# Turning x and xn by VectorE squares and DRAM instead of TensorE, in an adaLN block of linear attention and MLP

## The chip, the cores and the metric

The kernel runs on one core of one Trainium2 chip. The metric is the device time of one execution in microseconds (us); the median of several runs is given. About the profile: PE is TensorE's matmul, PEld its weight load (they overlap), DVE is VectorE, ACT ScalarE, POOL GpSimd, SP SyncE, whose queue issues the DMAs.

## The reference

One block with 2048 tokens and D = 576, 32 heads of 18, and an MLP of F = 4608:

```python
mod = (silu(c) @ w_mod)                      # six pieces: sa, ca, ga, sb, cb, gb
h = layernorm(x) * (1 + ca) + sa
q, k, v = split(h @ wqkv)                    # per head
pq, pk = phi(q), phi(k)                      # phi(t) = (t + 1 if t > 0 else exp(t)) + 1e-6
o = (pq @ (pk.T @ v)) / (pq @ sum(pk) + 1e-6)
x = x + ga * (o @ wo)
h = layernorm(x) * (1 + cb) + sb
x = x + gb * (silu(h @ w1) @ w2)
```

## The kernel before

Tokens are handled in 16 tiles of 128 (index `t`) and in 4 blocks of 512 (index `tb`); features in five chunks `k`, four of 128 and one of 64 columns, which is doubled to 128 by a copy of its columns (the "tail"). Every fp32 operand of a matmul is split into a high and a low fp32r part (a cast on ScalarE, a subtraction `sub_hi`, L121, on VectorE), and three passes are summed.

A matmul needs h with the features on partitions, and LayerNorm needs tokens on partitions, so each block of h is turned once. `transpose_chunk` (L214) does it on TensorE: four transposes of 128x128 against an identity for a chunk, into one bank of PSUM; then ScalarE applies shift and scale on the way out (`modulate`, L199), casts the high part (L205, L1093 or L869), and VectorE subtracts.

**First part (to about 206 us): projections.** After a head (0 to 40 us: the modulation's columns, LayerNorm and turning of block 0 of x), a loop over `t` runs `k_proj`, `v_proj`, `q_proj` (L226) and `kv_mm` (L589). In block `tb` it prepares block `tb + 1`: `load_x` (L260) loads four tiles with one DMA each at `t % 4 == 0`; statistics (L178), reciprocal deviation (L184 on POOL, L185) and normalisation (L191 on ScalarE for odd tiles, L193 on VectorE for even) at 1; `turn(tb + 1, k)` turns the chunks at 2 and 3, into `hT[tb + 1]`. `mod_piece` and `mod_col` (L526) make the later modulation. `load_wo` runs at `t == 10`.

**Second part (206 to about 368 us): attention output and the first group of the MLP.** `attn_step` (divide by the norm, turn, multiply by the folded kv and wo, add x, which was reloaded into `acc` by L756) goes over the 16 tiles; when a block is complete, its rows are normalised (`xn`, L191 and L193), and `turn_all(tb)` turns them by `turn_chunk_k` (L214), makes sums and differences of pairs of blocks (a seven-product scheme), splits them and stores them to DRAM (`hd`, L962). `mlp_units` (L886, L897) computes the MLP's first group of 256 hidden columns from each block and fills TensorE between.

**Steady state (from about 368 us):** the other 17 groups, with operands streamed back from `hd`, weights loaded and split, `up` matmuls (L1324), `down` matmuls (L1397) and VectorE additions (L1405). It runs in an order written in the code.

The order of the rest is given by `ORDERS`: for each engine a list of instruction numbers in program order, which `arrange` turns into dependencies of each instruction on the one before it. TensorE's list is nearly the program's own order.

## Time and profile before

| | |
|---|---|
| timed runs (3) | 1137.52, 1137.76, 1138.51 us; median 1137.76 |
| span of the profiled execution, first to last instruction | 1136.9 us |
| matmuls | 7033 |
| DMA packets, bytes | 58813, 269.03 MB |
| transposes on TensorE: of x blocks 1 to 3, of xn | 60, 80 |

Busy shares are given by the profile for each engine; a matmul's end is modelled, so neighbours overlap and a busy time for a group counts each instant once. A group's row reads: line, engine, operation, output and inputs by the program's names, shapes, count, then busy time and mean duration of one in ns, then the engine's idle time before such instructions and what ended it. In a row of stretches each engine's busy time is followed by the number of its instructions, and at the end stand TensorE's granted clock, the mean busy share of the 16 DMA engines and GB/s. A row of waits reads: total us, times, longest. A row of the timeline reads: start, duration (of several merged instructions the whole), engine, line, operation, count.

### The profile page before, as it was taken

Reading aid. Unit: us, or ns where it says so; the run is one execution under the profiler, and the core shown is the slowest. Engines: PE = TensorE matmul, PEld = TensorE weight load, DVE = VectorE, ACT = ScalarE, POOL = GpSimd, SP = SyncE. Lnnn points to the kernel's source line nnn. Section 1 sums busy time; section 2 is a strip of 40 time slices with the busy share of each in tenths; the row PEclk is TensorE's granted clock in tenths of the full one; section 3 lists DMA queues with packets and bytes.
Section 4 is the critical chain, followed back from the end, with each engine's and each line's share of the span. In section 5 each row is a group of like instructions: output and inputs, shape, how many; then the busy total and the mean of one; then the engine's idle time right before and its main releaser. Section 6 shows DMA issues by size and latency. Waiting matters only on the chain.

```text
span 1136.9 us, 19287 instructions
## 1 busy us (share of the span) xinstructions
PE 1126.8 (99%) x7033; PEld 1040.8 (92%) x7033; DVE 971.0 (85%) x1543; ACT 538.7 (47%) x1112; POOL 649.3 (57%) x743
## 2 busy tenths in 40 slices
PE   8999999999999999999999999999999999999998
PEld 7999999999998899999999999999989999999998
DVE  6866744686878899999999999999999999999996
ACT  5643442547556544445445444444444444444441
POOL 1100000374714777767775776677667767776786
PEclk9999999999999999999999999999999999999999
DMA  9621100223359877976978869779778697697684
GB/s 281 199 84 31 44 7 1 71 84 116 137 198 354 340 274 256 348 278 257 361 261 315 314 250 356 273 255 364 261 277 331 265 344 281 258 346 274 256 310 156
DMA packets 58813, 269.03 MB, mean 237 GB/s; under 512 B 5724, under 2 KB 21856, under 8 KB 35680
## 3 DMA queue, kind: packets, MB, share of 16 engines
q1 hardware_dynamic: 58708, 267.80, 64.4%
q8 instruction: 56, 0.92, 0.3%
q14 instruction: 37, 0.30, 0.1%
q10 hardware_dynamic: 12, 0.00, 0.0%
HBM read 250.12 MB, written 16.78 MB: 235 GB/s over the span
## 4 chain that ended last, share of the span: by engine, by line
PE 94%; DMA 3%; DVE 1%; ACT 1%; POOL 0%; SPq 0%; issue 0%; POOLq 0%
PE up L1324 34%; PE down L1397 32%; PE psK L226 12%; PE big L226 7%; PE small L886 2%; PE big L897 2%; PE kvp L589 1%; DMA hT<-in_w_mod_dram 1%; PE big L812 1%; DMA raw<-in_w_mod_dram 1%; DMA hT<-hd 1%; PE small L214 1%; DMA xt<-in_A_x_dram 1%; PE up L1427 1%; PE down L1427 1%; PE psT L214 1%
## 5 line engine op out<-in xcount | busy, mean ns | idle before, releaser
L1405 DVE TENSOR_TENSOR acc<-down,acc 128x576 f32<-128x576 f32 x330 | 246.2, 754 | 13.2 <-PE down L1397 3.2
L1324 PE MATMUL up<-hT,w 128*128 128x512 f32 x916 | 239.4, 390 | 0.5 <-DMA hT<-hd 0.5
L1324 PEld LDWEIGHTS up<-hT,w 128*128 128x128 f32 x916 | 164.5, 188 | 25.4 <-DMA hT<-hd 0.7
L1359 POOL TENSOR_TENSOR s<-f,f 128x256 f32<-128x256 f32 x66 | 52.3, 792 | 159.7 <-ACT f L1340 159.7
L1397 PE MATMUL down<-w,hb 128*128 128x288 f32 x792 | 120.6, 294 | 0.0
L1397 PE MATMUL down<-w,hc 128*128 128x288 f32 x792 | 120.6, 294 | 0.0
L1397 PEld LDWEIGHTS down<-w,hc 128*128 128x128 f32 x792 | 113.7, 188 | 5.4 <-PE up L1324 0.3
L1397 PEld LDWEIGHTS down<-w,hb 128*128 128x128 f32 x792 | 113.7, 188 | 5.3
L121 DVE TENSOR_TENSOR w<-v,w 128x288 fp32r<-128x288 f32 (+1 forms) x170 | 114.8, 684 | 2.8 <-ACT w L1058 2.8
L1405 DVE TENSOR_TENSOR U<-down,U 128x576 f32<-128x576 f32 x132 | 99.6, 754 | 17.1 <-PE down L1397 15.2
L226 PE MATMUL psK<-w,hT 128*128 128x352 f32 (+3 forms) x506 | 106.4, 336 | 1.1 <-POOL w L317 0.6
L1324 PE MATMUL up<-room,w 128*128 128x512 f32 x348 | 91.0, 390 | 0.0
L1378 POOL TENSOR_TENSOR hc<-s,hc 128x512 fp32r<-128x512 f32 x66 | 89.4, 1355 | 0.1
L184 POOL TENSOR_TENSOR rstd<-ve,neghalf 128x4 f32<-128x4 f32 (+3 forms) x10 | 9.5, 953 | 138.8 <-DVE ve L183 138.8
L226 PEld LDWEIGHTS psK<-w,hT 128*128 128x128 f32 x506 | 81.8, 188 | 7.5 <-POOL w L317 0.8
L1340 ACT ACTIVATE f<-f 128x512 f32<-128x512 f32 x102 | 64.5, 632 | 47.8 <-DVE f L1345 24.8
L1343 DVE TENSOR_TENSOR f<-up,p 128x512 f32<-128x512 f32 x102 | 69.7, 683 | 12.1 <-PE up L1324 11.2
L1066 ACT CAST w<-v 128x288 fp32r<-128x288 f32 x85 | 36.7, 434 | 76.4 <-PE down L1397 62.1
L1324 PEld LDWEIGHTS up<-room,w 128*128 128x128 f32 x348 | 62.5, 188 | 9.4
L1363 POOL TENSOR_TENSOR f<-f,s 128x256 f32<-128x256 f32 x66 | 51.2, 776 | 34.9 <-DVE hb L1378 24.5
L1397 PE MATMUL down<-w,he 128*128 128x288 f32 x396 | 63.0, 294 | 0.0
L1397 PE MATMUL down<-w,ha 128*128 128x288 f32 x396 | 63.0, 294 | 0.0
(310 smaller groups left out, 2529.7 us busy)
## 6 DMA issues: line engine op xcount, KB each, us to landing
hT<-hd SPq DMA_DIRECT2D x66, 1280.0 KB, 5.5
hT<-hd SPq DMA_DIRECT2D x45, 1024.0 KB, 5.5
room<-hd SPq DMA_DIRECT2D x35, 1280.0 KB, 5.7
room<-hd SPq DMA_DIRECT2D x20, 1024.0 KB, 5.1
v<-in_B_w_dram SPq DMA_DIRECT2D x17, 576.0 KB, 7.2
v<-in_B_w_dram SPq DMA_DIRECT2D x17, 512.0 KB, 7.1
hd<-S SPq DMA_DIRECT2D x6, 1024.0 KB, 3.8
xt<-in_A_x_dram SPq DMA_DIRECT2D x16, 288.0 KB, 5.2
```

Of the source, the lines that this page charges most:

```text
L121: return V.tensor_sub(lo, full, f32(hi))
L214: T.transpose(ps[:, i * P : (i + 1) * P], xt[i][:, cidx * P : (cidx + 1) * P], ident)
L226: T.matmul(ps, xpart(a), wpart(b), start=n == 0, stop=n == len(XW) - 1)
L1066: A.copy(self.w2[n][:, 0], src)
L1324: T.matmul(ps, left, right, start=first and m == 0, stop=m == len(seq) - 1, skip_group_check=True)
L1340: A.activation(self.f[i, k], self.f[i, k], AF.Silu)
L1343: V.tensor_add(f, self.bank[bank[1]], self.p1)
L1359: G.tensor_add(self.s[:, 0:1], half(i, 0, 1), half(i, 1, 1))
L1363: G.tensor_sub(half(i, 1, 0), half(i, 1, 0), self.s[:, 1:2])
L1378: eng.tensor_sub(t[:, :, 1, :], src, f32(t[:, :, 0, :]))
L1397: T.matmul(ps[:, p, :HALF], self.a[i, n][:, u, p * P : (p + 1) * P], self.w.w2[n][:, v], start=n in (1, 5, 7, 6) and j == 0, stop=j == 2, ...
L1405: V.tensor_add(dst, ps[:, :, :HALF], dst)
```

## The change

**x, blocks 1 to 3.** `load_x` loads each tile in four DMAs of 32 rows, so that partition group `a` of tile `i` holds rows `a*128 + 32*i` to `+31` of the block. After the normalisation (without the tail copy; ScalarE does all of block 1 and the odd tiles of the others) VectorE transposes squares of 32x32, one instruction of 128x576 for a tile, and four DMAs write the block to DRAM, feature by feature, in runs of 128 tokens (512 bytes). `turn` then loads a chunk's rows of 512 tokens (the tail chunk twice, 64 rows each), which lie in the block's own order, and modulates and splits as before. The staging rooms lie in `acc`'s tiles 8 to 15, now parts of one tile; therefore `load_wo` moves from `t == 10` to 12, and wq's split ahead of `v_proj(1)`.

**xn, blocks 0 to 2.** ScalarE normalises all four tiles, VectorE transposes each by squares, four DMAs write the block, and `turn_chunk_k` loads chunks instead of turning them. Here the tokens come in the order (partition group, tile, place), and the views `nat` and `box` put them back in the cast and the subtraction. Block 3 still goes through TensorE. Its sums with the others need the same order, so its modulation writes through these views.

**mod_col** multiplies by 32 columns of ones instead of 128.

**Orders.** The `ORDERS` of all engines are new for everything up to the steady state, TensorE's too, where matmuls of neighbouring steps now alternate. (`manual_schedule` for TensorE becomes `nullcontext`, with the table in its place.)

```diff
-            0-106 114 107-109 115 110-113 116-2586
+            0-1 37 2-7 9-13 38 14 8 39 15-16 40 17 41 21 18-19 42 22 25 20 26 29-36 51 43 45 44 46 49-50 47 56 48 57
...
-    accb = [accp.tile([P, 4, D], F32, name=f"acc{b}") for b in range(NB)]
-    acc = [accb[t // 4][:, t % 4, :] for t in range(NT)]
+    acca = accp.tile([P, NT, D], F32, name="acc")
+    accb = [acca[:, 4 * b : 4 * b + 4] for b in range(NB)]
+    acc = [acca[:, t, :] for t in range(NT)]
...
-        nc.sync.dma_start(xt[:, :D], x[(tb * 4 + i) * P : (tb * 4 + i + 1) * P, :])
+        if tb == 0:
+            nc.sync.dma_start(xt[:, :D], x[i * P : (i + 1) * P, :])
+        else:
+            for a in range(4):
+                r0 = tb * 512 + a * P + 32 * i
+                nc.sync.dma_start(xt[32 * a : 32 * a + 32, :D], x[r0 : r0 + 32, :])
...
-            T.matmul(ps[:, k * P : (k + 1) * P], t[:, k * P : (k + 1) * P], ones, start=True, stop=True)
+            T.matmul(ps[:, k], t[:, k * P : (k + 1) * P], ones[:, :32], start=True, stop=True)
...
+    free = acca[:, QB : NT, :].rearrange("p t d -> p (t d)")
+    squares = free[:, : 4 * D].rearrange("p (b i j) -> p b i j", i=4, j=32)
+    places = [free[:, (KC + 1 + n) * 512 :][:, :512] for n in range(4)]
+    xd = [dram.tile([D, 512], F32, name=f"xd{n}") for n in range(1 + NB)]
+
+    def turn_squares(xts):
+
+        for i in range(4):
+            V.transpose(squares[:, :, i, :], xts[i][:, :D].rearrange("p (b j) -> p b j", j=32))
+        for a in range(4):
+            rows = slice(32 * a, 32 * a + 32)
+            nc.sync.dma_start(xd[NB][:, a * P : a * P + P].rearrange("(b j) t -> j b t", j=32),
+                              squares[rows].rearrange("j b i t -> j b (i t)"))
+
+    def load_turned(dst, src, k):
+        if k < KC:
+            nc.sync.dma_start(dst, src[k * P : (k + 1) * P, :])
+        else:
+            for h in range(2):
+                nc.sync.dma_start(dst[h * 64 : h * 64 + 64], src[KC * P : D, :])
+
     def turn(tb, k):
-        ps = psT()
-        transpose_chunk(xts, k, ps)
-        h32 = pa.tile([P, 512], F32, name="h32")
-        modulate_split(ps, k, hT[tb], cols["a"], h32)
+        h32 = places[CHUNKS.index(k)] if k != 3 else pa.tile([P, 512], F32, name="h32")
+        load_turned(h32, xd[NB], k)
+        modulate_split(h32, k, hT[tb], cols["a"], h32)
...
-                    ln.normalise(j, xts[j], xts[j], A if j % 2 else V)
+                    ln.normalise(j, xts[j], xts[j], A if tb == 0 or j % 2 else V, False)
+                turn_squares(xts)
...
-            if t == 10:
+            if t == 12:
                 load_wo()
...
+    def nat(t):
+        return t.rearrange("p (a i j) -> p i a j", a=4, i=4)
+
+    def box(t):
+        return t.rearrange("p (i a j) -> p i a j", a=4, i=4)
...
     def turn_chunk_k(tb, k, h32):
-        ps = small()
-        transpose_chunk(xn2[tb], k, ps)
-        modulate(ps, k, None, cols["b"], h32, A)
+        if tb in SQUARES:
+            ps = h32
+            load_turned(h32, xd[tb], k)
+        else:
+            ps = small()
+            transpose_chunk(xn2[tb], k, ps)
...
-            hi, lo = hpart(tb, k, 0), hpart(tb, k, 1)
-            return A.copy(hi, h32), sub_hi(lo, h32, hi)
-        return tail_h(htail(tb), h32)
+            hi, lo = box(hpart(tb, k, 0)), box(hpart(tb, k, 1))
+            return A.copy(hi, nat(h32)), sub_hi(lo, nat(h32), hi)
+        return tail_h(box(htail(tb)), nat(h32))
...
+                y = pb.tile([P, D], F32, name="prod")
+                lns[tb].normalise(i, y, acc[4 * tb + i], A, False)
+                V.transpose(y4[:, :, i, :], y.rearrange("p (b j) -> p b j", j=32))
+            if tb in SQUARES:
+                for n in range(4):
+                    rows = slice(32 * n, 32 * n + 32)
+                    nc.sync.dma_start(xd[tb][:, n * P : n * P + P].rearrange("(b j) t -> j b t", j=32),
+                                      y4[rows].rearrange("j b i t -> j b (i t)"))
```

Three places in the order show what moved. TensorE at tile 2 of the first part, between its key projection (`psK_618` before, `psK_631` after) and its value projection (`psK_665`, `psK_673`); `xt_394` to `xt_400` are the four tiles of x block 1. Before:

```order
L226 MATMUL psK_618<-w_106,hT_102 128x352
L226 MATMUL psK_618<-w_106,hT_102 128x288
L214 MATMUL psT_656<-ident_85,xt_394 128x128
L214 MATMUL psT_656<-ident_85,xt_396 128x128
L214 MATMUL psT_656<-ident_85,xt_398 128x128
L214 MATMUL psT_656<-ident_85,xt_400 128x128
L226 MATMUL psK_665<-w_103,hT_102 128x512
```
The same place after, where `kvp` is the product of keys and values of an earlier tile:

```order
L668 MATMUL kvp0_105<-pk0_147,vx0_149 128x256
L299 MATMUL psK_631<-w_103,hT_99 128x352
L299 MATMUL psK_631<-w_103,hT_99 128x288
L299 MATMUL psK_673<-w_100,hT_99 128x512
L299 MATMUL psK_673<-v_101,hT_99 128x512
L299 MATMUL psK_673<-w_100,hT_99 128x512
L668 MATMUL kvp2_107<-pk0_147,vx0_149 128x128
L299 MATMUL psK_673<-w_100,hT_99 128x512
```
The four transposes are gone, and the kv products stand between the projections' matmuls instead of behind them.

VectorE, where the last step of x block 1's chunks stands, the subtraction that fills the low half of its `hT` (`hT_490` before, `hT_513` after). Before:

```order
L121 TENSOR_TENSOR hT_490<-h32_788,hT_490 128x512
L121 TENSOR_TENSOR pk1_151<-a_774,pk1_151 128x576
L121 TENSOR_TENSOR vx1_153<-psK_792,vx1_153 128x4x126
L121 TENSOR_TENSOR hT_490<-h32_816,hT_490 128x512
L334 SCALAR_TENSOR_TENSOR acc0_95<-e_732,acc0_95 128x576
L178 BN_STATS st_1030<-xt_863 128x6 x2
```
After, with `xt_853` to `xt_868` the tiles of block 2:

```order
L258 SCALAR_TENSOR_TENSOR nm_1031<-mv_1028,rstd_1030 128x4
L266 TENSOR_SCALAR xt_853<-xt_853,mv_1028,rstd_1030 128x576
L720 STREAM_TRANSPOSE acc_95<-xt_853 128x18x32
L266 TENSOR_SCALAR xt_863<-xt_863,mv_1028,rstd_1030 128x576
L193 TENSOR_TENSOR vx1_150<-psK_786,vx1_150 128x4x126
L720 STREAM_TRANSPOSE acc_95<-xt_863 128x18x32
L193 TENSOR_TENSOR vx1_150<-psK_786,vx1_150 128x8
L193 TENSOR_TENSOR hT_513<-acc_95,hT_513 128x512
L720 STREAM_TRANSPOSE acc_95<-xt_858 128x18x32
L193 TENSOR_TENSOR hT_513<-acc_95,hT_513 128x512 x2
```
Block 1's subtractions stood ahead of block 2's statistics; now they stand behind its statistics and its first two transposes.

SP in the second part, at xn block 2 (`hd` is where the MLP's operands are stored; `acc` is reloaded with x). Before:

```order
L756 DMA acc_98<-in_A_x_dram 128x576
L962 DMA hd_2343<-hT 128x512
L962 DMA hd_2339<-S 128x2048
L756 DMA acc_98<-in_A_x_dram 128x576
L962 DMA hd_2342<-S 128x2048
L962 DMA hd_2343<-S 128x2048
L962 DMA hd_2346<-hT 128x2560
```
After, with `xd2_388` the room in DRAM:

```order
L856 DMA acc_95<-in_A_x_dram 128x576
L1342 DMA xd2_388<-xn_3363 32x18x128 x4
L1062 DMA hd07_2314<-S_3297 128x2048
L728 DMA H_3562<-xd2_388 128x512
L731 DMA ht_3563<-xd2_388 64x512
```
Four writes and the loads back (six for a block) are new, and the loads stand ahead of reloads of x and of stores to `hd`.

More of the change, by code (lines that the diff above doesn't have):

```diff
@@ L1 @@
-from contextlib import ExitStack
+from contextlib import ExitStack, nullcontext
 from itertools import count
@@ L185, in finish, with normalise @@
             V.scalar_tensor_tensor(nm, self.mv[:, a:b, 0], -1.0, rstd, op0=ALU.mult, op1=ALU.mult)
-        def normalise(self, i, xt, r, eng):
-            for o, lo, hi in ((D, KC * P, D), (0, 0, D)):
+        def normalise(self, i, xt, r, eng, tail=True):
+            for o, lo, hi in ((D, KC * P, D), (0, 0, D))[not tail :]:
                 dst, src, rstd = xt[:, o : o + hi - lo], r[:, lo:hi], self.rstd[:, i : i + 1]
@@ L412, in warm_up @@
             T.matmul(o[:, 0:P], ones, ones, start=True, stop=True)
-    with tc.manual_schedule(engines={mybir.EngineType.PE}):
+    with nullcontext():
         V.memset(ones, 1.0)
@@ L537 @@
     NP0 = 2
+    QB = NT // 2
     def xsel(t):
@@ L648 @@
                 k_proj(t)
+            if t == 1:
+                for k in START:
+                    split_w(wqp_, k, acc[10 + k], V)
             if more and i == 1:
@@ L665 @@
                 turn_half((4,))
-                for k in START:
-                    split_w(wqp_, k, acc[10 + k], V)
             if more and i >= 2:
@@ L687 @@
                 tm = mod_piece(t // 3)
-            if t == 10:
+            if t == 12:
                 load_wo()
-    with tc.manual_schedule(engines={mybir.EngineType.PE}):
+    with nullcontext():
         qs = iter(range(QB, NT))
@@ L847, in load_mlp @@
         return w1, w2, wt
-    DIFF, ODD = 9, 5
+    DIFF, ODD, SQUARES = 9, 5, (0, 1, 2)
     h2 = {}
@@ L1547 @@
     units = [(g, p) for g in range(1, NG) for p in range(2)]
-    with tc.manual_schedule(engines={mybir.EngineType.PE}):
+    with nullcontext():
         fetch(5)
```

172 lines of the change are left out of this document (125 added, 47 removed).

## The prediction

> **What bounds the kernel now.** I read first the page's busy times, then who waited for whom on TensorE, then the busy times in four stretches: the head, the projections, the attention with the first MLP pair, and the rest.
>
> ```profile
> span 1136.9 us, 19287 instructions
> PE 1126.8 (99%) x7033; PEld 1040.8 (92%) x7033; DVE 971.0 (85%) x1543; ACT 538.7 (47%) x1112; POOL 649.3 (57%) x743
> ```
> ```profile
> PE psK L407 <- ACT hT L205: 1.3, 1, 1.3
> ...
> PE small L214 <- ACT H L199: 0.4, 1, 0.4
> ```
> ```profile
> core 0: us, PE busy (x) PEld busy (x) DVE busy (x) ACT busy (x) POOL busy (x), PEclk, DMA share, GB/s
> 0.00:40.00 40.00, 35.54 (x247) 33.28 (x248) 29.36 (x72) 27.22 (x55) 8.40 (x16) 1.00 0.79 240
> 40.00:206.00 166.00, 165.42 (x1084) 155.90 (x1083) 101.30 (x198) 66.63 (x133) 5.95 (x9) 1.00 0.19 56
> 206.00:368.00 162.00, 160.59 (x1139) 153.66 (x1139) 126.00 (x222) 96.51 (x173) 81.23 (x77) 1.00 0.46 161
> 368.00:1136.00 768.00, 765.30 (x4569) 697.98 (x4567) 714.30 (x1054) 348.34 (x752) 553.72 (x642) 1.00 0.78 292
> ```
> TensorE is busy for all but 10 us; its longest wait is 1.3 us, the longest before a transpose 0.4 us; its clock is full in every stretch. So work taken off TensorE shortens the kernel by its own length, as long as nothing that TensorE reads comes later than now. From 40 to 368 us, where the edits lie (the head only gets a new order), VectorE is busy for 101.30 of 166 and 126.00 of 162 us, ScalarE for less, and the DMA engines for 0.19 and 0.46 of the time: there is room. The steady state after 368 us has none on VectorE (714 of 768), but its instructions stay the same.
>
> **The part removed.** The transposes through TensorE, alone, in the same two stretches:
>
> ```profile
> core 0: us, PE busy (x) PEld busy (x), PEclk, DMA share, GB/s
> 40.00:206.00 166.00, 8.99 (x60) 7.35 (x60) 1.00 0.19 56
> 206.00:368.00 162.00, 11.72 (x80) 9.36 (x80) 1.00 0.46 161
> ```
> Blocks 1 to 3 of x are the 60 of the first: 9.0 us. Blocks 0 to 2 of xn are 60 of the 80 of the second: 11.72 x 60/80 = 8.8 us. Together **17.8 us**. Since TensorE is filled there, these busy times are its pace, not overlap.
>
> The narrower columns of `mod_col` I cost at nothing. Its 20 instructions stand beside 20 others of half the columns:
>
> ```profile
> L371 PE MATMUL kvp<-ones,hT 128*128 128x64 f32 x20 | 2.7, 280 | 0.1
> L526 PE MATMUL psK<-ones,tmod 128*128 128x128 f32 x20 | 2.6, 279 | 0.1
> ```
> 64 columns take as long as 128, so 32 will hardly take less; were the cost by the column, 2.0 of the 2.6 us would go. I keep that as an end only.
>
> **The part added.** No transpose of VectorE is in this trace. Its neighbours with 576 elements, and the steps of a chunk after it:
>
> ```profile
> L334 DVE SCALAR_TENSOR_TENSOR acc<-e,acc 128x576 f32<-128x576 f32 x16 | 13.6, 849 | 5.2 <-ACT acc L331 5.1
> L121 DVE TENSOR_TENSOR pk<-a,pk 128x576 fp32r<-128x576 f32 x16 | 12.1, 754 | 3.9 <-ACT pk L342 3.4
> L121 DVE TENSOR_TENSOR hT<-h,hT 128x512 fp32r<-128x512 f32 x15 | 10.3, 686 | 3.4 <-ACT hT L205 3.4
> L121 DVE TENSOR_TENSOR vx<-psK,vx 128x504 fp32r<-128x504 f32 x14 | 9.6, 682 | 6.2 <-ACT vx L544 6.2
> L193 DVE TENSOR_SCALAR xt<-xt,mv,rstd 128x576 f32<-128x576 f32 x7 | 3.8, 573 | 0.0
> ```
> ```profile
> L199 ACT ACTIVATE h<-psT,col_a 128x512 f32<-128x512 f32 x15 | 11.8, 786 | 1.6 <-PE psT L214 1.0 <-DVE vx L121 0.5 <-DVE hT L121 0.2
> L205 ACT CAST hT<-h 128x512 fp32r<-128x512 f32 x15 | 9.3, 622 | 0.3
> L191 ACT ACTIVATE xt<-xt,nm,rstd 128x576 f32<-128x576 f32 x9 | 7.6, 863 | 0.1
> ```
> One transpose then costs 0.57 to 0.85 us; I take 0.75, the row in the middle. Twelve in each stretch are 9 us of VectorE (6.9 to 10.2). In each stretch two normalisations leave VectorE for ScalarE (0.57 off, 0.86 on), and the copies of the tail columns go. VectorE's share becomes at most (101 + 8)/157 = 0.69 and (126 + 8)/153 = 0.88: still under TensorE. The views that put tokens back in order cost VectorE nothing by these rows (a subtraction of 512 plain elements 686 ns, of 504 in groups 682); for ScalarE I have no such row, and it has 0.4 of its time free. All of this is off the path as long as the operands come in time.
>
> What has to be in time is the way through DRAM. Rows for its DMAs (a stretch of the head, the queue and its issues, the loads of x):
>
> ```profile
> 2.00:14.00 12.00, 11.90 (x82) 11.35 (x82) 7.08 (x22) 5.47 (x10) 2.66 (x8) 1.00 0.97 291
> ```
> ```profile
> q1 hardware_dynamic: 58708, 267.80, 64.4%
> ...
> acc<-in_A_x_dram SPq DMA_DIRECT2D x16, 288.0 KB, 2.7
> ```
> ```profile
> L260 SPq DMA_DIRECT2D xt<-in_A_x_dram x16: 328/363/431, 0.8 to 123.5; - x16
> ...
> DMA to landing us min/median/max: 2.0/4.6/7.4
> ```
> A block is written in 4 x 32 x 18 = 2304 runs of 512 bytes, 144 for each of 16 engines. Between 2 and 14 us the loads, in rows of 1 KB and more, ran at 291 GB/s with 0.97 of the engines busy: 300/16 = 18.7 GB/s, or 55 ns for 1 KB. A run of 512 bytes takes 27 to 55 ns if it is like those: 3.9 to 7.9 us a block, with 2 us around it (the smallest landing) 6 to 10. The far end is the mean packet of the whole trace: 0.644 x 16 x 1136.9 us / 58708 = 0.20 us, so 31 us a block. I take 8, from the stage with the short rows. The loads back land 2.7 us after an issue of 0.36 us. The first chunk then passes 0.79 + 0.62 + 0.69 = 2.1 us of ScalarE and VectorE, each further one 1.4.
>
> The Trainium skill bears on that: "DMA: Bandwidth & Descriptors", section Specifications, names 512 bytes as the smallest transfer at line rate and about 358 GB/s as a core's limit to HBM, by which the 1.18 MB of a block would take 3.3 us, near my lower end. No trace so far has such runs by themselves.
>
> **Is there cover?** x block 1: its statistics are ready, and its first use begins, at
>
> ```profile
> 45.40 0.15 DVE L185 SCALAR_TENSOR_TENSOR nm<-mv,rstd 128x4 f32<-128x4 f32 x1
> ```
> ```profile
> 73.60 0.45 PE L226 MATMUL psK<-w,hT 128*128 128x352 f32 x2
> ```
> Less its 20 transposes (3 us) that leaves 25.2 us of TensorE work. The chain: four normalisations 3.5 and the last transpose 0.75; writing 8, in which SP also issues the 13 small loads that the order puts between (17 x 0.36 = 6.2 us, hidden); loads back 3.1; first chunk 2.1: 17.5 us (15.5 to 19.5), and 23.1 for the fifth chunk. It fits. The same points for xn's blocks 0, 1 and 2 (normalising begins, first matmul of the MLP):
>
> ```profile
> 252.67 1.44 ACT L191 ACTIVATE xn<-acc,nm,rstd 128x64 f32<-128x64 f32 x4 [3.01 <-DVE nm L185]
> 254.22 3.13 ACT L191 ACTIVATE xn<-acc,nm,rstd 128x576 f32<-128x576 f32 x4
> ...
> 279.23 0.43 ACT L191 ACTIVATE xn<-acc,nm,rstd 128x64 f32<-128x64 f32 x1
> ...
> 312.01 0.77 ACT L191 ACTIVATE xn<-acc,nm,rstd 128x64 f32<-128x64 f32 x2 [0.58 <-DVE nm L185]
> ```
> ```profile
> 275.34 1.54 PE L886 MATMUL small<-hT,w 128*128 128x512 f32 x6
> ...
> 307.42 1.55 PE L886 MATMUL small<-hT,w 128*128 128x512 f32 x6
> ...
> 339.16 3.22 PE small L886 x14
> ```
> Less 3 us each, 19.7, 25.2 and 24.2 us. The chain is 3.1 + 0.75 + 8 + 3.1 + 2.1 = 17.1 (15.1 to 19.1), the fifth chunk 22.7 after the start. Block 0 reads that chunk about 2.5 us into its 14 matmuls, at 22.2: the tight place, up to 2.5 us of wait; blocks 1 and 2 fit. I put 1.5 us of new waits in all, between 0 and 4.
>
> The loads back wait on SP for the four writes; the reloads of x for the attention's sums stand behind them, and the stores to `hd`. If the cover of those were gone, it would be a wait of the writes' 8 us at most; today no reload is among TensorE's waits.
>
> **Sum.** 1136.9 - 17.8 + 1.5 = 1120.6 for the execution profiled. The median of the timed runs, 1137.76, lies 0.86 above its span; with that, **1121.5 us**. With no new wait, `mod_col` at its end, and the 4.5 us gone that TensorE idles in the head (40 - 35.54), 1113.5; with 4 us of waits 1124.
>
> **Rivals.**
>
> *The order gives a part back.* VectorE now does the last step of block 1's chunks behind transposes of block 2, so TensorE's first use hangs on block 2's loads too: from 49.6 us, 16 small loads and four writes to issue (7.3), landing (4.6, at worst 7.4), then, by
>
> ```profile
> L178 DVE BATCH_NORM_STATS2 st<-xt 128x6 f32<-128x288 f32 x32 | 13.1, 440 | 5.0 <-DMA xt<-in_A_x_dram 5.0
> L184 POOL TENSOR_TENSOR rstd<-ve,neghalf 128x4 f32<-128x4 f32 x6 | 6.6, 1100 | 97.5 <-DVE ve L183 97.5
> ```
> some 2.5 us to the deviations, 3.5 for two normalisations, two transposes and what stands between, 0.7: 68.2 us, at worst 71.0, against a need at 70.6. If each of the four blocks above is 2 us late, 8 us are lost: 1129. For it: differences of 1 to 2 us decide. Against: TensorE's waits are short today under an order of the same kind. Chance 0.16.
>
> *Runs of 512 bytes are slow.* At 0.125 us a run, writing takes 20 us instead of 8; x block 1 waits 4.2 us, xn's blocks 9.4, 3.9 and 4.9: 22.4, more than the 17.8 saved, so 1142.4. From 0.117 us a run on it is slower than before; at 0.20, some 1185. For it: the mean packet takes 0.20 us. Against: that packet is nine times as long. In the Trainium skill, "VectorE: DVE Perf Modes", the section Rules for kernel authors sends a transpose of 128x128 to TensorE where PSUM will do, and The three transpose paths calls a plain DMA with transposing strides 19 times slower than the crossbar's; this rival is that rule at work. Chance 0.09.
>
> *The MLP's entry gives it back.* There the DMA engines are at their limit:
>
> ```profile
> 360.00:370.00 10.00, 10.00 (x65) 9.24 (x64) 9.96 (x16) 4.58 (x10) 3.80 (x5) 1.00 0.99 361
> ```
> The 2.36 MB of xn block 2, there and back, are 6.5 us at 361 GB/s; if they push the MLP's first operands by as much, 1128. Against: they pass some 30 us earlier. Chance 0.07.
>
> **The numbers.** The forecast, 1113.5 to 1124, has 0.66, and 0.02 is left for an order that loses the whole gain. 1115 to 1135 holds the first case without its corner and nearly all of the first and third rivals, 8 in 10 or a little more. About 0.2%, 2.3 us, is what a measurement can tell from no change. Faster by more: 0.66 + 0.13 + 0.06 = 0.85; slower by more: 0.10; between: 0.05.
>
> **What would show it.** 20 transposes are left on TensorE, its busy time is 18 us less, and its first use of x block 1 comes at 70 to 72 us. A transpose on VectorE takes about 0.75 us, and a block's writes land 6 to 10 us after the first is issued. I am wrong if TensorE waits over 4 us in all for `hT` and `small`, if the writes take over 15 us, or if its busy time falls by much less than its transposes.

## The result and the profile after

The changed kernel takes 1147.6 us (median of 6 runs, 1146.72 to 1149.05), the kernel before 1138.13 us (6 runs on the same chip). The ratio is 1.0074, interval 1.0054 to 1.0094: **slower by 0.7%**, where 1121.5 us, 1.4% faster, was forecast.

Span and busy times of the changed kernel:

```profile
span 1146.4 us, 19231 instructions
PE 1122.4 (98%) x6913; PEld 1028.8 (90%) x6913; DVE 981.0 (86%) x1555; ACT 537.5 (47%) x1100; POOL 650.7 (57%) x743
```

The 120 transposes are gone (7033 to 6913 matmuls). But TensorE's busy time fell by 4.4 us (from 1126.8), not by 18, and the time in which it stands still rose from 10.1 us (1136.9 - 1126.8) to 24.0. The four stretches of the prediction, TensorE alone (busy time, matmuls, clock, DMA share, GB/s):

```profile
core 0: us, PE busy (x), PEclk, DMA share, GB/s
0.00:40.00 40.00, 34.47 (x232) 0.96 0.73 216
40.00:206.00 166.00, 161.78 (x1032) 1.00 0.37 105
206.00:368.00 162.00, 152.01 (x1032) 1.00 0.57 186
368.00:1146.00 778.00, 774.13 (x4623) 1.00 0.78 293
```

TensorE, idle for 0.6 and 1.4 us of the second and third stretch before, is now idle for 4.2 and 10.0. The loss is made ahead of the steady state: the first `up` matmul starts at 367.9 us before and at 376.0 after (timelines, start and duration), 8.1 us later, and the span is 9.5 us longer:

```profile
367.89 2.89 PE L1324 MATMUL up<-first,w 128*128 128x512 f32 x12
```
```profile
376.01 0.63 PE L1448 MATMUL up<-first,w 128*128 128x512 f32 x2
```

Who waits for whom on TensorE (line and tile, what it waited for, total us, times, longest):

```profile
PE psK L485 <- ACT hT L278: 2.2, 2, 1.5
PE small L986 <- DVE hT L193: 2.0, 2, 1.1
PE psK L299 <- ACT wq L387: 1.6, 1, 1.6
...
```

No wait is long: many of 0.3 to 1.6 us, for results of ScalarE, VectorE and GpSimd of every kind. None is directly for a load from the room in DRAM. What is new in the path is about as fast as forecast. The transposes on VectorE (min/median/max ns), of x and of xn:

```profile
L720 DVE STREAM_TRANSPOSE acc<-xt x12: 733/768/780, 50.9 to 102.5; 128x576 f32<-128x576 f32 x12
```
```profile
L1338 DVE STREAM_TRANSPOSE xn<-prod x12: 772/778/779, 252.8 to 322.9; 128x576 f32<-128x576 f32 x12
```

The writes in runs of 512 bytes, and the loads back (KB of one, median us from issue to landing):

```profile
xd<-acc SPq DMA_DIRECT2D x12, 288.0 KB, 3.9
xd<-xn SPq DMA_DIRECT2D x12, 288.0 KB, 4.8
acc<-xd SPq DMA_DIRECT2D x9, 256.0 KB, 4.7
```

So three questions are left: why TensorE's busy time fell by a quarter of what was summed, where the new waits come from, and whether the path, the room that it uses or the new lists are to blame.

### The profile page after: what moved, and what is told of

Read it like the earlier page. It is cut to its first block, busy times and chain, and to the rows that moved or that the text cites. A ratio compares the mean times of both kernels' runs of the same rounds, so it can differ in the third digit from the quotient of the medians.

```text
span 1146.4 us, 19231 instructions
## 1 busy us (share of the span) xinstructions
PE 1122.4 (98%) x6913; PEld 1028.8 (90%) x6913; DVE 981.0 (86%) x1555; ACT 537.5 (47%) x1100; POOL 650.7 (57%) x743
## 4 chain that ended last, share of the span: by engine, by line
PE 79%; DVE 6%; ACT 2%; POOL 2%; DMA 2%; issue 1%; SPq 0%; POOLq 0%; DVEq 0%; ACTq 0%
PE up L1448 33%; PE down L1521 32%; PE psK L299 8%; PE big L299 2%; PE kvp L668 1%; ACT prod L264 1%; DVE S L193 1%; DVE xn L1338 1%; DVE hT L193 1%; PE up L1551 1%; PE down L1551 1%; POOL pn L853 1%; DMA hd<-hT 1%; DVE acc L1002 0%; DVE acc L926 0%
## 5 line engine op out<-in xcount | busy, mean ns | idle before, releaser
L1448 PE MATMUL up<-hT,w 128*128 128x512 f32 x916 | 243.1, 390 | 0.1
L299 PE MATMUL psK<-w,hT 128*128 128x512 f32 (+3 forms) x506 | 116.2, 341 | 1.4 <-DVE a L411 1.2
L1529 DVE TENSOR_TENSOR U<-down,U 128x576 f32<-128x576 f32 x132 | 99.5, 754 | 16.2 <-PE down L1521 14.2
L299 PE MATMUL big<-w,qT 128*128 128x288 f32 x352 | 66.2, 303 | 1.8 <-DVE acc L926 1.3
L1521 PE MATMUL down<-w,hd 128*128 128x288 f32 x396 | 64.1, 294 | 0.0
```

The costliest lines, as they stand in the source:

```text
L299: T.matmul(ps, xpart(a), wpart(b), start=n == 0, stop=n == len(XW) - 1)
L1448: T.matmul(ps, left, right, start=first and m == 0, stop=m == len(seq) - 1, skip_group_check=True)
L1521: T.matmul(ps[:, p, :HALF], self.a[i, n][:, u, p * P : (p + 1) * P], self.w.w2[n][:, v], start=n in (1, 5, 7, 6) and j == 0, stop=j == 2, ...
L1529: V.tensor_add(dst, ps[:, :, :HALF], dst)
```

## The experiments

All ratios are to the kernel before, run beside it on the same chip; where runs that were not made side by side are compared, it is by their ratios, and 0.001 is 1.1 us. A line of `...` in a code cut marks what is left out; of a list of numbers only the first line is shown.

**One suspect at a time.** First theories: TensorE's alternating order costs matmul pace; the way through DRAM comes late; the one tile `prod` in which the rows of xn are normalised and turned holds up GpSimd, which needs it for the attention's products. The last shows in the changed kernel's view of that tile (first lines: how long and when; last: who waited for it, us, times):

```profile
L1309 POOL TENSOR_TENSOR prod<-acc,z x14: 1412/1432/1801, 222.3 to 326.4; 128x576 f32<-128x576 f32 x14
...
  POOL prod L1309: 25.9, 9
```

and in the same view of before:

```profile
L1196 POOL TENSOR_TENSOR prod<-acc,z x14: 1425/1434/2556, 222.0 to 290.9; 128x576 f32<-128x576 f32 x14
...
  POOL prod L1196: 11.9, 8
```

GpSimd waits 25.9 us for the tile instead of 11.9, and the last product starts at 326.4 us instead of 290.9.

*e1*, TensorE's list alone back to (nearly) the program's order:

```diff
-            0-1 37 2-7 9-13 38 14 8 39 15-16 40 17 41 21 18-19 42 22 25 20 26 29-36 51 43 45 44 46 49-50 47 56 48 57
...
+            0-1669 1671-1698 1670 1699-2466
```

> The changed kernel with TensorE's list back in the program's order (one matmul, number 1670, stands 28 places later, since the other engines' lists need it so); the lists of the other engines stay as changed. Theory O (TensorE's alternating order costs the gain: 1071 changes of group instead of 463 before 410 us, with weight loads and short waits in the open): the matmuls' extra time up to 410 us falls by about 10 us, so 1134 to 1140 us. Theory R (the way through DRAM is late): TensorE meets the turned chunks no later than now, so the time stays within 1145 to 1150. Theory S (the attention's product waits for a room that the normalised rows now share): order does not help, 1145 to 1150, or slower, since the other lists were made for the alternating one.

Measured: 1173.85 us, ratio 1.0299 (1.0269 to 1.0328). TensorE's waits for GpSimd's `pn` (the attention's operand, divided by the norm) in that run, and around its longest wait the engines' timelines:

```profile
PE big L845 <- POOL pn L788: 6.0, 2, 3.4
PE big L845 <- POOL pn L786: 4.9, 3, 3.5
```
```profile
259.48 0.87 ACT L197 ACTIVATE prod<-acc,nm,rstd 128x576 f32<-128x576 f32 x1 [6.42 <-DVE nm L191]
...
261.96 0.63 ACT L341 ACTIVATE acc<-big 128x576 f32<-128x576 f32 x1
```
```profile
262.69 1.30 PE L845 MATMUL big<-ident,pn 128*128 128x128 f32 x5 [6.65 <-issue]
```

Undoing the alternation, with the other engines' lists left as they are, costs 26 us: in the program's order TensorE stands in front of the matmuls that turn `pn`, for 10.9 us until GpSimd has it. The one wait of 6.65 us has no releaser in the profile; it ends 0.1 us after ScalarE has read a tile `big`, and the matmul writes one; ScalarE stood for 6.42 us before, in front of the normalisation of xn. So that wait is more likely for the room than for `pn`. The alternation is a remedy for operands and rooms that come late, not the cause.

*e2*, rows of xn normalised and turned in their own room:

```diff
-                y = pb.tile([P, D], F32, name="prod")
-                lns[tb].normalise(i, y, acc[4 * tb + i], A, False)
-                V.transpose(y4[:, :, i, :], y.rearrange("p (b j) -> p b j", j=32))
+                y = y4[:, :, i, :]
+                A.activation(y, acc[4 * tb + i].rearrange("p (b j) -> p b j", j=32), AF.Identity,
+                             bias=lns[tb].nm[:, i : i + 1], scale=lns[tb].rstd[:, i : i + 1])
+                V.transpose(y, y)
```

> The changed kernel, but the normalised rows of xn's blocks 0 to 2 are written straight to the room of the squares and turned there in place, so that they no longer pass through the one room that the attention's product uses; all lists stay. Theory S: GpSimd's product waited 18.7 us in three waits for VectorE's transposes; without them the attention's operands come earlier and TensorE's idle time from 220 to 360 us (about 11 us) falls by 3 to 8 us: 1140 to 1145. Theory O: the lists keep the product where they put it, within 2 us of 1147.6. Theory R: within 2 us as well.

Measured: 1146.59 us, ratio 1.0062 (1.004 to 1.0084). Against the change's 1.0074 that is 1.4 us less, and within the intervals nothing. The theory of the shared room falls for the kernel as it is ordered.

*e3*, the loads back take rows of w1 that lie in DRAM from the start, so that they wait for no write:

```diff
-            nc.sync.dma_start(dst, src[k * P : (k + 1) * P, :])
+            nc.sync.dma_start(dst, B_w1[k * P : (k + 1) * P, 0:512])
...
```

> The changed kernel, but the loads back take rows of B_w1 of the same shape and length instead of the turned x and xn, so they do not wait for the writes (the values are then other ones). Theory R: the chunks come 10 us and more earlier, and the time falls by 3 us or more, towards 1138. Theories O and S: TensorE's waits do not hang on these loads, so within 2 us of 1147.6.

Measured: 1147.65 us, ratio 1.0074 (1.0045 to 1.0103), the changed kernel's own. Waiting for the round trip through DRAM costs nothing in this order that a ratio known to 0.003 can show; that theory falls.

*e4*, the edits of e1 and e2 together.

> Both: rows turned in place, and TensorE in the program's order. Theory O alone: as the run with the order alone. Theory S with O: faster than either alone, 1128 to 1136, since the product no longer holds up the attention and TensorE no longer changes group at nearly every matmul. Theory R: 1145 to 1150.

Measured: 1173.92 us, ratio 1.0312 (1.0274 to 1.0351), as e1 alone. The shared room does not explain why `pn` is late either.

**The new path in the old order.** Four kernels in which every engine's list follows the start times recorded of before; instructions that before doesn't have come as soon as what they read is there:

```diff
-            0-1 37 2-7 9-13 38 14 8 39 15-16 40 17 41 21 18-19 42 22 25 20 26 29-36 51 43 45 44 46 49-50 47 56 48 57
...
+            0-106 114 107-109 115 110-113 116-2466
...
-            2 0 6 5 7-8 12 11 4 13 1 14 10 18 16 15 17 9 19-21 3 22 29 23 28 24 30 25-27 44 31 43 34 33 36-37 35 32 38
...
+            0 3 2 1 4 6-7 11 8 12-13 9-10 14-16 18 17 5 19-22 30 23-24 28-29 25-27 43 31 44 33-34 36 35 37-38 32
...
```

*e5*, with the rooms of e2:

> The changed data path (x by squares as changed, xn turned in place in the squares' room), but all five lists anew: every instruction that the kernel before has too stands where it started there by its trace, and the new ones stand as early as their operands allow. Theory L (the lists are what costs: they were made for an attention that starts late and interleave TensorE finely): TensorE loses the 120 transposes and keeps its old order and its old distance to its operands, so 1121 to 1128. Theory P (the new data path itself holds TensorE up, by the early split of wq, the late wo and the squares' rooms): 1138 to 1146 in any order.

*e6*, with the shared room:

> The changed kernel with nothing but the lists replaced, in the same way as in the run with the old order on the new path: the normalised rows still pass through the one room of the attention's product. Theory L without the room: as that run, 1121 to 1128. Theory S with L (the room forces the product of the next steps behind four normalisations and transposes, whatever the lists): 5 us or more slower than that run, with TensorE waiting for pn after each of the first three blocks.

*e7*, x by squares alone, xn through TensorE:

```diff
-    DIFF, ODD, SQUARES = 9, 5, (0, 1, 2)
+    DIFF, ODD, SQUARES = 9, 5, ()
```

> Only x's blocks 1 to 3 go by squares and DRAM; xn's four blocks are turned by TensorE as before; lists by the order of before. Theory L: 9.0 us of transposes less and no new wait: 1128 to 1132. Theory P: the early split of wq and the late wo cost at least the 9 us: 1136 to 1144.

*e8*, xn by squares alone, x through TensorE (x's loads, wq's split and `load_wo` as before):

```diff
...
-        h32 = places[CHUNKS.index(k)] if k != 3 else pa.tile([P, 512], F32, name="h32")
-        load_turned(h32, xd[NB], k)
-        modulate_split(h32, k, hT[tb], cols["a"], h32)
+        ps = psT()
+        transpose_chunk(xts, k, ps)
+        h32 = pa.tile([P, 512], F32, name="h32")
+        modulate_split(ps, k, hT[tb], cols["a"], h32)
...
```

> Only xn's blocks 0 to 2 go by squares (turned in place) and DRAM; x is turned by TensorE as before; lists by the order of before. Theory L: 8.8 us of transposes less, at most 2 us of waits for the first block's chunks: 1128 to 1133. Theory P: the chunks come too late for the MLP and the sums, 1136 to 1144.

Measured:

| | us | ratio |
|---|---|---|
| e5 | 1200.71 | 1.0558 (1.0539 to 1.0576) |
| e6 | 1226.0 | 1.0775 (1.0758 to 1.0791) |
| e7 | 1181.39 | 1.0386 (1.0366 to 1.0407) |
| e8 | 1175.99 | 1.0333 (1.0312 to 1.0354) |

In the old order the new path costs 63 us; x's part alone costs 44, xn's alone 38, so the two do not add up. Who TensorE waits for in e5:

```profile
PE psK L231 <- DVE vx L125: 15.1, 4, 11.7
PE big L844 <- DVE qT L125: 10.5, 4, 8.9
PE psK L231 <- DVE col_b L538: 10.3, 1, 10.3
```

None of these is a step of the new path. Ahead of the wait for `vx`, VectorE's only idle piece from 66 to 82 us (idle time and its releaser in brackets) and, behind it, ScalarE's longest wait from 60 to 82 us:

```profile
74.22 0.69 DVE L125 TENSOR_TENSOR hT<-acc,hT 128x512 fp32r<-128x512 f32 x1 [13.21 <-ACT hT L210]
```
```profile
ACT acc L204 <- DMA acc<-xd: 15.9, 1, 15.9
```

VectorE stands for 13.2 us in front of a chunk's subtraction, since ScalarE stands for 15.9 in front of the load back. The cast of `vx`, which needs nothing of that chunk, stands behind it in ScalarE's list and starts at 74.10 us; the subtraction of `vx` stands behind the chunk's in VectorE's and starts at 76.16; TensorE goes on at 79.91, after 11.70 us. This is the mechanism of the prediction's first rival at a larger size: an engine takes its list strictly in turn, and one step with a long chain holds up what has nothing to do with it. Here the shared room costs 25 us (e6 against e5): what order hides in the changed kernel it does not hide here. So the change could not have kept the old lists with the new steps as early as their operands allow; no other placement in them was tried.

**How much was there to gain?** *e9* is the kernel before without the 120 transposes and with nothing in their place.

```diff
-        ps = psT()
-        transpose_chunk(xts, k, ps)
+        ps = xts[k % 4][:, :512]
...
-        ps = small()
-        transpose_chunk(xn2[tb], k, ps)
+        if tb < 3:
+            ps = xn2[tb][k % 4][:, :512]
+        else:
+            ps = small()
+            transpose_chunk(xn2[tb], k, ps)
```

> The kernel before without the 120 transposes on TensorE and with nothing in their place: the modulation of x's blocks 1 to 3 and of xn's blocks 0 to 2 reads the normalised rows as they lie, unturned, so the values are other ones; all lists are those of before. It measures the gain that was there to be had, with no new path in the way. Theory G (the gain is there, 17.8 us as the prediction summed it, and the changed kernel loses it and more elsewhere): 1138.1 - 17.8 = 1120.3 us, 1118 to 1124, TensorE's busy time down by 17 to 19 us. Theory N (the transposes were mostly filling: without them TensorE waits for VectorE's or ScalarE's next operand instead): 1130 us or more, TensorE's idle time up from 10 us to over 18 us.

Measured: 1130.56 us (1127.98 to 1132.38), ratio 0.9924 (0.9902 to 0.9946): a gain of 8.7 us (6 to 11 by the interval), not 17.8. Span and busy times, and TensorE's first waits:

```profile
span 1128.8 us, 19043 instructions
PE 1115.1 (99%) x6913; PEld 1028.2 (91%) x6913; DVE 968.9 (86%) x1543; ACT 538.6 (48%) x1112; POOL 648.9 (57%) x743
```
```profile
PE up L1326 <- DMA room<-hd: 1.8, 3, 1.3
...
PE big L226 <- DVE qT L121: 1.2, 1, 1.2
...
PE big L226 <- DVE acc L825: 0.9, 2, 0.7
```

The time is where the theory of waits put it, but the idle time is not (13.7 us, where over 18 were expected), and neither is the busy time where the other put it: both have a part. TensorE's busy time fell by 11.7 us, not by 17.8, and its idle time rose by 3.6 us, to 13.7: new are waits for the attention's `qT` and `acc`, and for `room`, an operand of the steady state. The first part is a matter of reading. A place in the timeline of before (start, duration of all together), four transposes and the matmuls behind them:

```profile
54.77 0.60 PE L214 MATMUL psT<-ident,xt 128*128 128x128 f32 x4
55.12 1.06 PE L589 MATMUL kvp<-pk,vx 128*128 128x256 f32 x7
```

Four transposes are busy for 0.60 us, 150 ns each, as in the prediction (8.99/60). But the next matmul starts 0.35 us after the first of them: they hold TensorE for 88 ns each. The rest of each one's 272 ns (the median in the view of L214) lies under its successor. From the first start to what follows, all 30 groups of four take 12.8 us, two waits of 0.9 us in all included. Weight loads overlap less: their busy time fell by 12.6 us (1040.8 to 1028.2), close to what the spacing gives, and the prediction's own row had 7.35 + 9.36 x 60/80 = 14.4 us of it for these 120. The Trainium skill, "Perfetto Trace Analysis", section Identifying the Most-Contended Engine, says that matmul busy time tells poorly how near TensorE is to its limit, matmuls being pipelined, and takes the busy time of the weight loads instead. These traces agree: by weight loads the prediction would have had 14.4 us where it had 17.8, and 12.6 us of them went.

**Lists or path?** *e10* is the changed kernel with all its lists and each instruction in its place, but with a path that costs next to nothing.

```diff
-            V.transpose(squares[:, :, i, :], xts[i][:, :D].rearrange("p (b j) -> p b j", j=32))
+            V.transpose(squares[:, :1, i, :], xts[i][:, :32].rearrange("p (b j) -> p b j", j=32))
...
-            nc.sync.dma_start(xd[NB][:, a * P : a * P + P].rearrange("(b j) t -> j b t", j=32),
-                              squares[rows].rearrange("j b i t -> j b (i t)"))
+            nc.sync.dma_start(xd[NB][:32, a * P : a * P + P].rearrange("(b j) t -> j b t", j=32),
+                              squares[rows, :1].rearrange("j b i t -> j b (i t)"))
...
-            nc.sync.dma_start(dst, src[k * P : (k + 1) * P, :])
+            nc.sync.dma_start(dst, B_w1[k * P : (k + 1) * P, 0:512])
...
-                y = pb.tile([P, D], F32, name="prod")
-                lns[tb].normalise(i, y, acc[4 * tb + i], A, False)
-                V.transpose(y4[:, :, i, :], y.rearrange("p (b j) -> p b j", j=32))
+                y = y4[:, :, i, :]
+                A.activation(y, acc[4 * tb + i].rearrange("p (b j) -> p b j", j=32), AF.Identity,
+                             bias=lns[tb].nm[:, i : i + 1], scale=lns[tb].rstd[:, i : i + 1])
+                V.transpose(y[:, :1], y[:, :1])
...
-                    nc.sync.dma_start(xd[tb][:, n * P : n * P + P].rearrange("(b j) t -> j b t", j=32),
-                                      y4[rows].rearrange("j b i t -> j b (i t)"))
+                    nc.sync.dma_start(xd[tb][:32, n * P : n * P + P].rearrange("(b j) t -> j b t", j=32),
+                                      y4[rows, :1].rearrange("j b i t -> j b (i t)"))
```

> The changed kernel with its lists, every instruction in its place, but the new path made nearly free: rows normalised and turned in their own room; each transpose on VectorE is one square row of 128x32 instead of 128x576; each write to DRAM moves 32 runs instead of 576; the loads back take rows of w1 and wait for no write. The values are other ones. Theory P (the path's own work, transposes, writes, room, costs the time): it falls from 1146.6 us (own room alone) towards 1125, at least below 1137. Theory L (the lists cost it, whatever the path does): within 3 us of 1146.6, so 1143 to 1149, with the same scattered waits on TensorE before 380 us.

Measured: 1144.54 us (1142.34 to 1147.26), ratio 1.0049 (1.0033 to 1.0066). The theory of the lists holds, if the instructions that the path adds to the lists are counted with them: their number and places are kept, and the loads back have their full size. The profile looks like that of the changed kernel:

```profile
span 1145.0 us, 19222 instructions
PE 1121.2 (98%) x6913; PEld 1029.2 (90%) x6913; DVE 970.1 (85%) x1555; ACT 536.6 (47%) x1100; POOL 649.2 (57%) x743
```
```profile
PE small L986 <- DVE hT L193: 3.1, 2, 2.0
PE psK L299 <- DVE a L411: 2.5, 1, 2.5
PE psK L299 <- ACT wq L387: 2.2, 1, 2.2
...
```

Against e9, run beside it, TensorE does the same 6913 matmuls, and the ratio is 0.0125 higher, 14.2 us. In the profiled executions TensorE idles 23.8 us instead of 13.7, and is busy for 6.1 us more. Its busy time from 0 to 40, 40 to 206 and 206 to 368 us is 32.40, 163.93 and 152.33 us, in e9 35.79, 165.53 and 157.68. So about half of the added idle time lies ahead of 206 us, 3.4 us of it in the head, where the new path has not begun: the new order of the head costs something by itself.

Of the added busy time more than half is the clock, which falls to half in two places of e10's execution and stays at 1.00 in e9's (stretches of 2 us):

```profile
44.00:46.00 2.00, 2.00 (x11) 0.58 0.16 23
```
```profile
312.00:314.00 2.00, 2.00 (x9) 0.50 0.99 410
```

With their neighbours (0.57 from 42 us; 0.98 from 310 and 0.66 from 314) full speed is withheld there for 3.4 us, nearly all of it while TensorE works. (The two of e10's eight executions with a mean clock of 0.997, this one among them, take 1146.8 and 1147.3 us, the others 1142.3 to 1144.9.) The other 2.7 us can follow from the waits: a matmul of 128x288 is listed with 297 ns, but in a row of them one starts every 0.135 us (e9's timeline, start and duration of 19 together, (2.73 - 0.30)/18):

```profile
54.47 2.73 PE L226 MATMUL psK<-wq,hT 128*128 128x288 f32 x19
```

The 0.16 us that else lie under the next one show as busy time whenever there is no next one in time; 2.7 us are some 17 such places, an estimate from these rows.

*e14* asks which engine's list it is: e10 with TensorE's list as in e1.

```diff
-            0-1 37 2-7 9-13 38 14 8 39 15-16 40 17 41 21 18-19 42 22 25 20 26 29-36 51 43 45 44 46 49-50 47 56 48 57
...
+            0-1669 1671-1698 1670 1699-2466
```

> The kernel of e10 (the changed kernel's lists, path nearly free, 1144.5 us) with TensorE's list alone put back to the program's order, as in e1. The values are other ones. Theory A (TensorE's alternating order is what costs the changed kernel its time once nothing is waited for): below 1138. Theory V (VectorE's, ScalarE's and GpSimd's lists put the attention's operands late, and the alternation makes that good): 1160 or more, with waits for pn on TensorE again.

Measured: 1171.93 us, ratio 1.0304 (1.0287 to 1.0322). With nothing to wait for on the path, TensorE stands in front of the same matmuls again, for `pn` and once, as in e1, with no releaser shown:

```profile
PE big L845 <- issue: 7.4, 1, 7.4
PE big L845 <- POOL pn L788: 5.9, 2, 3.5
```

So the other engines' lists put the attention's operands late, whether the path takes time or not. In e10, with no shared room and a path nearly free, the products still run from 220 to 325 us (222 to 291 before), and GpSimd waits 24.6 us for the tile (11.9 before), now for VectorE's sums over it (`den`), which stand late in VectorE's list:

```profile
L1309 POOL TENSOR_TENSOR prod<-acc,z x14: 1417/1434/1966, 220.0 to 325.4; 128x576 f32<-128x576 f32 x14
L849 DVE TENSOR_REDUCE den<-prod x14: 699/742/755, 223.7 to 327.0; 128x32 f32<-128x576 f32 x14
...
  POOL prod L1309: 24.6, 7
```

*e13* asks the same of the old order: e5 with the path made nearly free by the edits of e10.

> The kernel of e5 (rows turned in their own room, all lists by the recorded start times of before; 1200.7 us), with the path made nearly free as in e10: transposes of 128x32, writes of 32 runs, loads back that take rows of w1 and wait for no write. The values are other ones. Theory C (in the old order it is the length of the chain through DRAM that in-order lists cannot wait for): it falls by 50 us or more, to 1150 or below, and the waits for vx, col_b and qT of over 8 us go. Theory I (the instructions added to SP, ScalarE and VectorE do it, whatever they wait for): it stays above 1180.

Measured: 1172.02 us, ratio 1.03 (1.0284 to 1.0317). Neither number was met: 29 us of e5's 63 go, 34 stay. Where VectorE waits now ahead of `vx`, and what SP issues before the load that ScalarE waits for:

```profile
71.08 0.69 DVE L125 TENSOR_TENSOR hT<-acc,hT 128x512 fp32r<-128x512 f32 x1 [9.49 <-ACT hT L210]
```
```profile
58.68 1.76 SPq L270 DMA_DIRECT2D xt<-in_A_x_dram  x4
...
61.11 1.92 SPq L270 DMA_DIRECT2D xt<-in_A_x_dram  x4
...
63.97 2.33 SPq L660 DMA_DIRECT2D acc<-in_B_w_dram  x3
```

The load waits for no write, but it is issued only at 64.0 us, behind eight small loads of the next block in SP's queue, and VectorE's subtraction still holds up the rest. The queue and the list are a cost of their own.

**The same rule for both.** Would a better order bring the gain? *e11* and *e12* have lists made by one rule from the same recorded execution, for the kernel before and for the changed kernel with the rooms of e2. TensorE's list of e12 begins so:

```diff
-            0-1 37 2-7 9-13 38 14 8 39 15-16 40 17 41 21 18-19 42 22 25 20 26 29-36 51 43 45 44 46 49-50 47 56 48 57
...
+            0-7 9-18 37-42 8 19-20 29-36 21-24 51-52 72 25-28 53 73 78-81 43-46 66-69 47-50 54-65 70-71 74-77
...
```

> The kernel before, data path unchanged, with lists for the part up to the steady state made anew by one rule: at each point an engine takes, of what is ready, what came first in the recorded execution, and small shifts of that are tried. It is the yardstick for the next run, whose lists come from the same rule. All theories: within 1% of 1138.1, since the rule starts from this kernel's own order.

> The changed kernel with rows turned in their own room and with lists made by the rule of the run before this one, starting from the same recorded execution. Theory L (the changed kernel's lists cost the gain, the path itself is worth about 17 us less small waits): below the run before this one by 8 us or more. Theory P (the path, by the length of its chain, takes the gain back under any list): no faster than the run before this one, or slower. Between, both share it.

Measured: e11 1156.06 us, ratio 1.0153 (1.0131 to 1.0176); e12 1166.43 us, ratio 1.0243 (1.022 to 1.0266). The yardstick itself missed its 1%, so the rule is worse than the lists of before, and both lose part of it in the head (end of this text). But like against like, the new path is 0.009, some 10 us, slower again; up to 4 us of that is the clock (mean of the execution 0.985 to 0.990 in e12, 0.991 in e11). In three ways of ordering (the change's lists, the recorded order, this rule) it loses, by 8, 63 and 10 us. No version was found that beats both kernels.

## Why the prediction was wrong, point by point

- **"Since TensorE is filled there, these busy times are its pace, not overlap" failed.** The 17.8 us removed were worth 8.7 (e9). The transposes' pace was 88 ns in the place shown, not 150, and the weight loads had it: 12.6 us. The rest, some 4 us, was lost since TensorE, sooner at the attention and at the steady state, finds operands that are not there yet. "Its longest wait is 1.3 us" was true of the old pace only; the prediction did not ask by how much the operands were ahead. Its own sign of being wrong, a busy time that falls by much less than the transposes, came: 4.4 us in the changed kernel.
- **"I put 1.5 us of new waits in all, between 0 and 4" failed, and with it the place of the risk.** The prediction looked for waits at the new path's ends. There e3 finds none that go away when the loads wait for no write. What cost 14.2 us (e10 against e9) are the new lists and what moves with them, which the prediction put at nothing as long as operands come no later. They begin in the head, they spread the attention's operands over the second part, and TensorE's alternation makes good 29 us of what they would cost (e14 against e10) but not all.
- **The rival "The order gives a part back" was the right kind, at a wrong place and size.** It named one chunk's subtraction in the first part and 8 us; in the old order such single holds are 9 to 13 us long (e5), and the lists that avoid them pay in many small waits. The 0.02 for an order that loses the whole gain was far too little: with a gain of 8.7 us, an order that costs 14 is enough.
- **The path itself held.** The transpose was put at 0.75 us and takes 0.77 to 0.78; the writes of a block at 8 us, and in xn's block 0 the first load back is issued 6.9 us after the first write (258.78 and 265.71 us), in x's block 1, with ten loads of the next block between, 10.2 us after it (55.68 and 65.88). "Runs of 512 bytes are slow" falls. (The 19 times that the prediction cites from the Trainium skill, "VectorE: DVE Perf Modes", section The three transpose paths, is said there of a large innermost stride at the destination; these writes have 512 contiguous bytes innermost, so it did not bear on them.) The first use of x block 1 does not come at 70 to 72 us, but later than before (73.6):

```profile
74.72 0.53 PE L299 MATMUL psK<-w,hT 128*128 128x352 f32 x2 [0.25 <-DVE vx L193]
```
  By ratios, path and shared room together cost 0.0025 over e10, some 2.8 us, of two ratios that are each known to about 2 us: near the 1.5 that was put there.
- **`mod_col`** at nothing was not tried by itself.
- **The MLP's entry** gives back a little in e9: the first `up` matmul starts 9.8 us sooner (358.1 instead of 367.9), the end comes 8.1 sooner, with 1.8 us of waits for `room`.
- **The sum by what was measured:** -8.7 (transposes gone), +14.2 (lists and moves), +1.5 (path, e2 against e10), +1.4 (shared room, the change against e2) = +8.4 us, the ratio of 1.0074. These are differences along one chain of kernels, so they add up by construction. The last two are inside their intervals.

Open is which entries of VectorE's, ScalarE's and GpSimd's lists cost the 14 us, how much of it is the added instructions, the early split of wq and the new order of the head, which e10 keeps, and whether lists exist that hide the path without them. That the path does not fit the old lists as e5 and e13 place its steps is shown; that every order must cost so much is not. That the part of TensorE's added busy time which is not the clock is the overlap lost at each wait is worked out, not tried.

## What to carry to other kernels

Price what leaves TensorE by the distance from its first matmul's start to the start of what follows, or by its weight loads, not by busy time; and before building its replacement, time the kernel with the work simply left out: here that one run put the gain with the old lists at 8.7 us. A longer chain for an operand costs little where it ends and much in the lists: each in-order engine and DMA queue that it passes must be reordered, and everything else on them moves too. When a change comes with new lists for all engines, the lists are the change: look at the steps that the data path doesn't touch.

## What the runs showed of the hardware

A transpose of squares in its own room (output on input) takes its time like any other: e2 ran with all 12 of xn so, at a median of 778 ns, as in the change. Writes of 512-byte runs were no slower to land (3.9 and 4.8 us) than loads back in rows of 2 KB (4.7).

TensorE's granted clock can halve after a short wait, but does not after each. In the changed kernel's head one wait of 1.47 us ends at 23.5 us (timeline: start, duration, idle time before it in brackets), and behind it the clock is 0.50 (stretches of 2 us: TensorE's busy time, matmuls, clock, DMA share, GB/s):

```profile
23.48 1.91 PE L485 MATMUL psK<-w,hT 128*128 128x288 f32 x7 [1.47 <-ACT hT L278]
```
```profile
22.00:24.00 2.00, 0.53 (x4) 0.91 1.00 263
24.00:26.00 2.00, 2.00 (x10) 0.50 0.63 175
26.00:28.00 2.00, 2.00 (x13) 0.73 0.68 183
```

The kernel before, whose longest wait is 1.3 us, keeps 1.00 throughout. But e10 has the same wait of 1.47 us in its head (to 22.6 us) and one of 2.51 us (to 30.1 us) with the clock at 1.00, and falls to half only behind one of 2.21 us (to 41.8 us). In e11, waits of 0.69, 1.34 and 0.86 us between 9 and 13 us are followed by some 10 us at half clock, which withhold full speed for 5 us, more than the waits themselves. The Trainium skill, "TensorE: Matmul & The Clock Gate", section HAM oscillation — how this bites in real kernels, warns of idle gaps of over about 3.4 us; here a gap of 1.47 us was followed by half clock once, and one of 2.51 us was not.

In the changed kernel's profiled execution these rows come to 1.7 us of full speed withheld, and from 40 us on its clock is 1.00 again, so this explains little of its 9.5 us. In the slower experiments it weighs more. The mean clock of an execution is 0.998 to 1.00 in the kernel before and in e9, 0.996 to 0.999 in the change, e2, e3 and e10, 0.985 to 0.988 in e1, e4 and e14, and 0.973 to 0.979 in e5. At 0.979, e5's 1198.7 us lack 25 us of full speed; as TensorE stood still in part of that time, this is the most that it can have cost. So some of what is put down to waits above, in e1, e5, e13 and e14 above all, is the half clock that follows them.
